# Expert loop of a pooled-attention and top-1 MoE kernel: another order of the four arms, an aligned loop head and a branch hint

## The chip, the cores and the metric

One core of one Trainium2 chip. The metric is device time in microseconds (us), the median of the timed runs. A profiled execution lies beside them, with a trace of each engine's instructions: PE (TensorE, the matrix engine), PEld (its weight loads, from the same sequencer), DVE (VectorE), ACT (ScalarE), POOL (GpSimd), SP (SyncE, here the issuer of most DMAs).

## The reference

Attention with keys and values averaged over groups of 8 positions, then a mixture of experts in which each token goes to its one best expert:

```python
k_p = k.reshape(B, H, Sp, pool, D).mean(axis=3)          # B, H, S, D = 8, 8, 576, 64; pool = 8
v_p = v.reshape(B, H, Sp, pool, D).mean(axis=3)
attn = softmax(scale * q @ k_p^T)
x = (attn @ v_p).transpose(0, 2, 1, 3).reshape(B * S, H * D)     # 4608 tokens of 512
expert_idx = argmax(x @ w_gate)                                   # 8 experts
for e in range(E):
    h = np.maximum(x_sorted[lo:hi] @ w1[e], 0.0)                  # 512 -> 1024
    y_sorted[lo:hi] = h @ w2[e]                                   # 1024 -> 512
return gate_w[:, None] * y_sorted[inv_perm]
```

(softmax and the sorting by expert are abridged.)

## The kernel before

The attention part, up to some 200 us, is written out in full; it scatters each token's row into a DRAM table `x_by_expert`, sorted by expert. The expert part works in blocks of up to 256 tokens of one expert. Its first block is computed in the straight code; all others run in a loop over `T` blocks, where `T` and a small table (`tabs`) come from the routing that was computed just before. Here the loop makes 21 passes.

Matmuls are done in float16 with values split into a high and a low part, three products for each float32 product. The weights of an expert, split likewise, lie in one of two slots: slot 0 (`w` in the trace) and slot 1 (`qt` for w1, `kv` for w2). Experts take the slots in turn. While the blocks of one expert are computed, the next one's weights are loaded into a staging buffer (by SP, `wwhole`) and split into the other slot (by ACT and DVE, `part` and `wsplit`, L116 and L118).

A block that holds at most 128 tokens does half the work. So there are four arms: slot 0 or 1, whole or half block. A table entry `code` picks one: 0 is slot 0 half, 1 is slot 0 whole, 2 is slot 1 half, 3 is slot 1 whole. Each arm is a call of `block(s, full, en)` and holds the code of PE, ACT and DVE for it; POOL and SP have no code in the arms. On PE an arm has the up part (`up`, lines L1005 to L1007: 96 matmuls of 256 columns, or 128 in a half block, into the PSUM tiles ps, pp and pq) and the down part (`finish`, L1082: 48 matmuls of 512 columns, or 24). Between them ACT makes the relu's high part (`relu_hi`, L1073) and DVE the low part (`relu_lo`, L1076). With them in each arm: DVE's copy of the next block's transposed tokens (`arrive`, L931), the split of the tokens of the block after it (`split_hi` and `split_lo`, L913 and L916), and ACT's scaled result (`take`, L1247), which POOL scatters to the output (`give`, L1252).

The order of the work within an arm is the order of the Python calls (the schedule is manual). The head of the loop body loads `code` and `en` into registers (L1221) and branches twice (L1309, in `either`). The loop is of the kind in which semaphores are never reset: waits compare with registers that count up. Its closing branch is L1314 in the trace, and each engine executes a prefetch hint for that branch (BRANCH_PREFETCH_HINT, shown under L1359) at the top of each pass.

Each engine has a sequencer that reads its instructions, executes branches, register operations and waits by itself, and hands the others to the engine. The trace has rows for both.

Of the kernel before, what the change touches and what calls it, by code (L numbers as in the profile page):

```python
# [15 lines left out]
ENG = mybir.EngineType  # L16
# [16 lines left out]
def kernel(  # L33
# [51 lines left out]
    def wwhole(e, stage):  # L85

        for src, dst in zip((w1d, w2d), WHOLE[stage]):
            src = src[e:e + 1] if isinstance(e, int) else src[ds(e, 1)]
            nc.sync.dma_start(dst, src.rearrange("e p c f -> p (e c) f"))
# [806 lines left out]
    def keep_ids(x=xg):  # L896
        pass_ids(gC, iC, x[:, :, ID + 1], x[:, :, ID].bitcast(I32))
        nc.gpsimd.tensor_tensor(x[:, :, ID].bitcast(I32), far.to_broadcast([128, 2]), zi.to_broadcast([128, 2]), op=OP.add)

    def move_ids():  # L900
        pass_ids(gA, iA, gC, iC)

    def take_ids():
        pass_ids(gB, iB, gA, iA)
# [13 lines left out]
    def split_x():  # L918
        split_hi()
        split_lo()  # L920
# [5 lines left out]
    def trans():  # L926
        nc.sync.dma_start(xTs.rearrange("p (c t) -> p c t", c=4 * DC), xh.rearrange("p j a t -> p (j a t)"),  # L927
                          transpose=True)

    def arrive():  # L930
        nc.vector.tensor_copy(xT.rearrange("p c (j t) -> p j c t", j=2),  # L931
                              xTs.rearrange("p (j c t) -> p j c t", j=2, c=2 * DC))
# [67 lines left out]
    def up(s, f, n):  # L1000
        dst = pH[f // 2][:, (f % 2) * BLK:(f % 2) * BLK + n]
        c = slice(f * 128, (f + 1) * 128)
        for d in range(DC):
            wh, wl = W1[s][0][:, d, c], W1[s][1][:, d, c]
            nc.tensor.matmul(dst, wh, xT[:, d, 0:n], start=(d == 0), stop=False)  # L1005
            nc.tensor.matmul(dst, wh, xT[:, DC + d, 0:n], start=False, stop=False)  # L1006
            nc.tensor.matmul(dst, wl, xT[:, d, 0:n], start=False, stop=(d == DC - 1))  # L1007
# [64 lines left out]
    def relu_hi(k, n=BLK):  # L1072
        nc.scalar.activation(pair(hT[0], k, n), ups_of(k, n), AF.Relu)  # L1073

    def relu_lo(k, n=BLK):
        V.scalar_tensor_tensor(pair(hT[1], k, n), ups_of(k, n), 0.0, pair(hT[0], k, n), op0=OP.max, op1=OP.subtract)  # L1076

    def finish(s, j, half):
        y = pY[j]
        for x, z in (((0, 0), (0, 1), (1, 0)), ((0, 0), (1, 0), (0, 1)))[half]:  # L1080
            for f in range(4 * half, 4 * half + 4):
                nc.tensor.matmul(y, hT[x][:, f, 128 * j:128 * j + 128], W2[s][z][:, f, :],  # L1082
                                 start=(half == x == z == f == 0), stop=(half == z == 1 and f == FC - 1))
# [6 lines left out]
    rest = [f for _, _, f in fillers]  # L1090
# [128 lines left out]
    def entry(kind, t, engines, lo, hi):  # L1219
        ap = tabs[kind:kind + 1, t:t + 1] if isinstance(t, int) else tabs[kind:kind + 1, ds(t, 1)]  # L1220
        return nc.values_load(ap, engines=engines, min_val=lo, max_val=hi)  # L1221

    def load_x(t, x=xg):
        row = entry(0, t, [ENG.SP], 0, E * SEG - 128)
        many = entry(4, t, [ENG.SP], 0, 3)

        def part(lo, n, dst):
            src = xs[ds(row + lo, n), :]
            st = nc.sync.dma_start(dst, src if n < BLK else src.rearrange("(j p) x -> p j x", p=128))
            if isinstance(t, int):  # L1230
                for e, o in padded:
                    if e > t + 1:
                        tc.declare_no_dep(st.ins, o.ins, reason="rows of later experts")

        with tc.If(many > 2) as cmp:
            part(0, BLK, x)
        with cmp.Else():
            part(0, 64, x[0:64, 0])
            with tc.If(many > 0):
                part(64, 64, x[64:128, 0])  # L1240
                with tc.If(many > 1):
                    part(128, 64, x[0:64, 1])
# [3 lines left out]
    def take(j):  # L1246
        nc.scalar.activation(ys[j], pY[j], AF.Copy, scale=gB[:, j:j + 1])  # L1247

    def give(j):
        nc.gpsimd.tensor_tensor(iG[:, 0:j + 1], iB[:, 0:j + 1], zi.to_broadcast([128, j + 1]), op=OP.add)  # L1250
        nc.gpsimd.tensor_tensor(spacer[:, 0:1], ys[j][0:1, 0:1], iG[0:1, j:j + 1].bitcast(F32), op=OP.add)  # L1251
        st = nc.gpsimd.indirect_dma_start(  # L1252
            out=out, out_offset=bass.IndirectOffsetOnAxis(ap=iG[:, j:j + 1], axis=0), in_=ys[j], in_offset=None,
            bounds_check=N - 1, oob_is_err=False)
        for o in given:
            tc.declare_no_dep(st.ins, o.ins, reason="rows of other tokens")
        given.append(st)
# [22 lines left out]
    T = nc.values_load(tab[0:1, 0:1], min_val=1, max_val=TMAX)  # L1280
# [4 lines left out]
    def part(s, en):  # L1285
        with tc.If(en > 0):
            for j in range(8):
                wsplit(1 - s, j, "hl", s)

    def block(s, full, en):  # L1290
        for h in range(2):
            n = BLK if full else 128
            for f in range(4 * h, 4 * h + 4):
                up(s, f, n)
            for k in (2 * h, 2 * h + 1):
                relu_hi(k, n)
                relu_lo(k, n)
        arrive()
        split_x()
        part(s, en)  # L1300
        if full:
            for half in range(2):
                finish(s, 1, half)
        take(1)
        for half in range(2):
            finish(s, 0, half)

    def either(c, f, g):
        with tc.If(c) as cmp:  # L1309
            f()  # L1310
        with cmp.Else():
            g()

    with tc.For_i(0, T, 1, iteration_sync="reg_based") as t:  # L1314
        code = entry(6, t, [ENG.PE, ENG.Activation, ENG.DVE], 0, 3)
        en = entry(2, t, [ENG.Activation, ENG.DVE], 0, 1)
        en3 = [entry(x, t, [ENG.SP], 0, E - 1) for x in (7, 3)]
        more = [entry(5, t + x, [ENG.SP], 0, 1) for x in (2, 3)]
        take_ids()
        move_ids()  # L1320
        keep_ids()
        nc.gpsimd.drain()
        either(code < 2,
               lambda: either(code > 0, lambda: block(0, True, en), lambda: block(0, False, en)),
               lambda: either(code > 2, lambda: block(1, True, en), lambda: block(1, False, en)))
        with tc.If(more[0] > 0):
            trans()
        with tc.If(more[1] > 0):
            load_x(t + 3)
        give(1)  # L1330
        for x in (0, 1):
            with tc.If(en3[x] > 0):
                wwhole(en3[x], 1 - x)
        take(0)
        give(0)
# [28 lines left out]
```

## Time and profile before

| | |
|---|---|
| timed runs, us | 617.01, 619.32, 626.0 (median 619.32) |
| profiled execution, us | 623.24 |
| its span, first to last instruction, us | 621.3 |
| PE busy | 573.8 us, 92% |
| DVE, ACT, POOL busy | 50%, 47%, 43% |
| loop, first to last matmul, us | 215.34 to 613.8 |
| mean granted clock of PE | 0.982 |

Busy time is the time in which an engine has an instruction in work; branches, waits and register operations don't count. Matmuls overlap in the pipeline: a row's duration is longer than the distance to the next one, and it is the distance from start to start that adds up. [...]

### The profile page before, as it was taken

The page shows a single profiled execution, that of the slowest core. Times are in us where ns is not written, and L with a number is a line of the kernel's source. Part 1 is how long each engine was busy: PE and PEld are TensorE (multiplying, and loading weights), DVE is VectorE, ACT ScalarE, POOL GpSimd, SP SyncE. Part 2 cuts the span into 40 slices and gives each one's busy share as a digit, 9 for nine tenths or more (in the row PEclk, how much of TensorE's full clock was granted, in tenths as well). Part 3 has the DMA queues.
Part 4 walks back from the last instruction along what each step waited for, and adds up shares of the span by engine and source line. Part 5 has one row for each costly group of instructions (what it writes and reads, how often), then busy time and mean ns, then how long its engine had stood idle before and what let it go on. Part 6 is the DMA issues. An engine that isn't in the chain of part 4 may idle for free. (4 is left out here: it accounts for less than half of the span.)

```text
span 621.3 us, 15783 instructions
## 1 busy us (share of the span) xinstructions
PE 573.8 (92%) x4721; PEld 420.5 (68%) x4722; DVE 313.1 (50%) x625; ACT 291.6 (47%) x648; POOL 269.9 (43%) x524
## 2 busy tenths in 40 slices
PE   6798889999887899998999999999999999999995
PEld 5787878888775366655667666767666666567663
DVE  6567888987965336224772772213722461222122
ACT  2487779899951135225652772223522441222122
POOL 5799398997986153211332332122311132111213
PEclk9699999999999799999999999999999989999999
DMA  8996698976397547954888579243332324321200
GB/s 233 309 307 206 220 294 290 294 242 218 120 310 208 140 106 211 399 132 92 266 250 269 168 249 338 72 106 80 77 89 51 87 55 106 89 51 53 68 17 31
DMA packets 96323, 107.15 MB, mean 172 GB/s; under 512 B 54430, under 2 KB 64670, under 8 KB 96288
## 3 DMA queue, kind: packets, MB, share of 16 engines
q1 hardware_dynamic: 89648, 85.72, 49.0%
q0 software_dynamic: 6640, 20.99, 9.2%
q8 instruction: 19, 0.31, 0.2%
q14 instruction: 16, 0.13, 0.1%
HBM read 72.99 MB, written 23.37 MB: 155 GB/s over the span
## 5 line engine op out<-in xcount | busy, mean ns | idle before, releaser
L1082 PEld LDWEIGHTS <-bd 128*128 128x128 f16 x936 | 91.6, 98 | 113.5 <-issue 7.9
L1251 POOL TENSOR_TENSOR spacer<-ql,iG 1x1 f32<-1x1 f32 x44 | 20.3, 462 | 206.1 <-ACT ql L1247 196.9
L1076 DVE SCALAR_TENSOR_TENSOR bd<-ps,bd 128x512 f16<-128x512 f32 (+1 forms) x44 | 27.5, 630 | 158.6 <-ACT bd L1073 154.8
L516 ACT ACTIVATE both<-ps,nmx 128x72 f32<-128x72 f32 x288 | 68.6, 327 | 12.8 <-DVE nmx L509 12.0
L1082 PE MATMUL po<-w,bd 128*128 128x512 f16 x264 | 58.9, 379 | 0.0
L1082 PE MATMUL po<-kv,bd 128*128 128x512 f16 x264 | 58.8, 379 | 0.0
L1073 ACT ACTIVATE bd<-ps 128x512 f16<-128x512 f32 (+1 forms) x44 | 24.0, 548 | 71.2 <-PE L1005 42.4
L1252 POOL DMA_INDIRECT out_dram<-ql,iG x44 | 46.2, 1049 | 21.4 <-issue 20.3
L1082 PE MATMUL pq<-w,bd 128*128 128x512 f16 x192 | 46.5, 394 | 4.4 <-issue 3.5
L1082 PE MATMUL pq<-kv,bd 128*128 128x512 f16 x216 | 48.1, 379 | 0.0
L499 PE MATMUL ps<-bd,qT 128*128 128x144 f32 x256 | 46.2, 305 | 1.6 <-DVE bd L785 0.9
L1005 PE MATMUL ps<-kv,qt 128*128 128x256 f16 (+1 forms) x176 | 45.6, 267 | 2.1 <-issue 2.1
L1007 PE MATMUL ps<-kv,qt 128*128 128x256 f16 (+1 forms) x176 | 45.7, 267 | 2.0 <-DVE qt L118 2.0
L1006 PE MATMUL ps<-kv,qt 128*128 128x256 f16 (+1 forms) x176 | 45.6, 267 | 0.0
L1007 PE MATMUL ps<-kv,w 128*128 128x256 f16 (+1 forms) x176 | 43.1, 258 | 1.9 <-DVE w L118 1.9
L1005 PE MATMUL ps<-kv,w 128*128 128x256 f16 (+1 forms) x176 | 43.1, 258 | 1.6 <-DVE kv L118 1.5
L1006 PE MATMUL ps<-kv,w 128*128 128x256 f16 (+1 forms) x176 | 43.1, 258 | 0.0
L1247 ACT ACTIVATE ql<-po,gB 128x512 f32<-128x512 f32 x22 | 15.0, 684 | 58.7 <-PE L1005 33.8
L709 POOL DMA_INDIRECT x_by_expert<-both,rpos x36 | 35.4, 985 | 14.7 <-issue 5.9
L1005 PEld LDWEIGHTS <-qt 128*128 128x128 f16 x352 | 34.7, 99 | 8.2 <-issue 2.6
L1007 PEld LDWEIGHTS <-qt 128*128 128x128 f16 x352 | 34.7, 99 | 7.3 <-issue 3.2
L1005 PEld LDWEIGHTS <-w 128*128 128x128 f16 x352 | 34.4, 98 | 6.3 <-ACT kv L116 2.0
(250 smaller groups left out, 1361.1 us busy)
## 6 DMA issues: line engine op xcount, KB each, us to landing
both<-in_moe_w_dram SPq DMA_DIRECT2D x6, 2048.0 KB, 11.6
st<-in_moe_w_dram SPq DMA_DIRECT2D x6, 2048.0 KB, 14.5
vb<-x_by_expert SPq DMA_DIRECT2D x16, 578.0 KB
st<-in_moe_w_dram SPq DMA_DIRECT2D x8, 1024.0 KB
kv<-in_k_dram SPq DMA_DIRECT2D x7, 1024.0 KB
kv<-in_v_dram SPq DMA_DIRECT2D x7, 1024.0 KB
qt<-in_q_dram SPq DMA_DIRECT2D x6, 1024.0 KB
qt<-in_q_dram SPq DMA_DIRECT2D x4, 512.0 KB
```

The costliest lines, as they stand in the source:

```text
L499: nc.tensor.matmul(ps[:, x * 2 * KP:(x + 1) * 2 * KP], t[:, h, :], BD[b % 3][:, :, h, :], start=True, stop=True)
L516: nc.scalar.activation(p[:, h * KP:(h + 1) * KP], ps[:, x * KP:(x + 1) * KP], AF.Exp, bias=nmx[:, x:x + 1], scale=-1.0)
L709: st = nc.gpsimd.indirect_dma_start(out=xs, out_offset=bass.IndirectOffsetOnAxis(ap=Z["pos"][:, u:u + 1], axis=0), in_=X[:, u, :], in_offs ...
L1005: nc.tensor.matmul(dst, wh, xT[:, d, 0:n], start=(d == 0), stop=False)
L1006: nc.tensor.matmul(dst, wh, xT[:, DC + d, 0:n], start=False, stop=False)
L1007: nc.tensor.matmul(dst, wl, xT[:, d, 0:n], start=False, stop=(d == DC - 1))
L1073: nc.scalar.activation(pair(hT[0], k, n), ups_of(k, n), AF.Relu)
L1076: V.scalar_tensor_tensor(pair(hT[1], k, n), ups_of(k, n), 0.0, pair(hT[0], k, n), op0=OP.max, op1=OP.subtract)
L1082: nc.tensor.matmul(y, hT[x][:, f, 128 * j:128 * j + 128], W2[s][z][:, f, :], start=(half == x == z == f == 0), stop=(half == z == 1 and f ...
L1247: nc.scalar.activation(ys[j], pY[j], AF.Copy, scale=gB[:, j:j + 1])
L1251: nc.gpsimd.tensor_tensor(spacer[:, 0:1], ys[j][0:1, 0:1], iG[0:1, j:j + 1].bitcast(F32), op=OP.add)
L1252: st = nc.gpsimd.indirect_dma_start(out=out, out_offset=bass.IndirectOffsetOnAxis(ap=iG[:, j:j + 1], axis=0), in_=ys[j], in_offset=None, b ...
```

## The change

The choice among the four arms is made in another order: first whether `code` is 1 (whole block of slot 0), and only otherwise among the other three. In the code the three other arms come first (slot 0 half, slot 1 half, slot 1 whole), and the whole-block arm of slot 0 comes last, directly in front of the loop's end. The branch that leads to it gets the label "rest". At the head of the body PE executes a hint for that branch, whose value is computed from the pass number: `(t + 63) // 64` is 0 in the first pass ("likely taken") and 1 in all later ones ("likely not taken"). And the first instruction of the loop body on PE is placed at the start of a block of instruction fetch. What the arms compute, and the order within an arm, stay as they are. The order of the arms changes for PE, ACT and DVE; the hint and the alignment are for PE alone.

```diff
-    def either(c, f, g):
-        with tc.If(c) as cmp:
+    def either(c, f, g, label=None):
+        with tc.If(c, label=label) as cmp:
             f()
         with cmp.Else():
             g()
 
-    with tc.For_i(0, T, 1, iteration_sync="reg_based") as t:
+    with tc.For_i(0, T, 1, iteration_sync="reg_based", head_align_engines=[ENG.PE]) as t:
+        tc.mark_branch_hint_location("rest", hint=(t + 63) // 64, engines=[ENG.PE])
         code = entry(6, t, [ENG.PE, ENG.Activation, ENG.DVE], 0, 3)
...
-        either(code < 2,
-               lambda: either(code > 0, lambda: block(0, True, en), lambda: block(0, False, en)),
-               lambda: either(code > 2, lambda: block(1, True, en), lambda: block(1, False, en)))
+        either(code != 1,
+               lambda: either(code < 1, lambda: block(0, False, en),
+                              lambda: either(code < 3, lambda: block(1, False, en), lambda: block(1, True, en))),
+               lambda: block(0, True, en), "rest")
```

## Rows read from the trace of the kernel before

**Rows 1.** The page: busy us of each engine (share of the span), instructions.

```profile
PE 573.8 (92%) x4721; PEld 420.5 (68%) x4722; DVE 313.1 (50%) x625; ACT 291.6 (47%) x648; POOL 269.9 (43%) x524
```

**Rows 2.** Stages of the loop: length, busy us (instructions), PE clock, DMA share, GB/s.

```profile
215.34:236.20 20.86, 20.86 (x144) 13.97 (x144) 8.79 (x10) 9.68 (x13) 8.48 (x18) 1.00 0.54 116
...
237.88:258.71 20.83, 20.83 (x144) 14.08 (x145) 7.89 (x9) 5.57 (x9) 7.98 (x16) 1.00 0.91 329
...
281.85:293.39 11.54, 11.51 (x120) 7.90 (x121) 4.78 (x8) 5.36 (x9) 1.99 (x9) 1.00 0.22 63
293.39:316.38 22.99, 21.36 (x145) 13.88 (x144) 19.06 (x20) 17.44 (x22) 6.32 (x14) 1.00 0.89 259
316.38:326.90 10.52, 10.52 (x121) 7.69 (x120) 5.81 (x9) 3.97 (x7) 5.56 (x12) 1.00 0.80 258
```

**Rows 3.** Waits of PE, 209 to 300 us, then 300 to 621 us: total, times, longest.

```profile
PE ps L1005 <- issue: 2.1, 1, 2.1
PE ps L1007 <- DVE w L118: 1.6, 3, 0.6
PE ps L1005 <- DVE kv L118: 1.5, 1, 1.5
...
PE ps L1007 <- DVE qt L118: 2.0, 4, 0.5
```

**Rows 4.** PE's branches, windows 232:233 and 277.7:278: ns min/median/max, first and last start.

```profile
L1309 PEldq COMPARE_BRANCH  x1: 3549/3549/3549, 232.3 to 232.3; - x1
...
L1309 PEldq COMPARE_BRANCH  x2: 366/2012/3659, 277.4 to 277.8; - x2
```

**Rows 5.** The same view: 283:611 (both lines), 254:255 and 491:493.

```profile
L1309 PEldq COMPARE_BRANCH  x50: 71/186/228, 291.3 to 601.6; - x50
...
L1314 PEldq COMPARE_BRANCH  x17: 231/231/245, 290.0 to 599.9; - x17
...
L1309 PEldq COMPARE_BRANCH  x1: 202/202/202, 254.8 to 254.8; - x1
...
L1309 PEldq COMPARE_BRANCH  x1: 186/186/186, 491.9 to 491.9; - x1
```

**Rows 6.** DMA queues 212:232, 232:237, 277:283.5 (packets, MB, share), first of 283.5:621.

```profile
q8 instruction: 2, 0.03, 0.7%
...
q8 instruction: 1, 0.02, 1.6%
...
q8 instruction: 2, 0.03, 1.9%
...
q1 hardware_dynamic: 43296, 33.16, 35.9%
```

**Rows 7.** PE's sequencer at loop entry, and its hints in all passes.

```profile
L1314 PEldq COMPARE_BRANCH  x1: 376/376/376, 212.5 to 212.5; - x1
...
L1309 PEldq COMPARE_BRANCH  x2: 71/87/103, 214.3 to 214.4; - x2
...
L1359 PEldq BRANCH_PREFETCH_HINT  x21: 31/36/52, 212.9 to 600.2; - x21
```

**Rows 8.** PE in time, fourth pass: start us, us, what [idle before].

```profile
281.85 0.22 PE L1005 MATMUL ps<-kv,qt 128*128 128x128 f16 x1 [2.14 <-issue]
...
283.52 0.22 PE L1005 MATMUL ps<-kv,qt 128*128 128x128 f16 x1
...
284.19 0.22 PE L1005 MATMUL ps<-kv,qt 128*128 128x128 f16 x1
```

**Rows 9.** PE in time, loop entry, and the end of a half block of slot 0.

```profile
213.77 1.46 PE L1082 MATMUL po<-w,bd 128*128 128x512 f16 x6
215.34 0.28 PE L1005 MATMUL ps<-kv,w 128*128 128x256 f16 x1
...
494.61 0.27 PE L1005 MATMUL ps<-kv,qt 128*128 128x256 f16 x1
```

**Rows 10.** ACT in time, the first relu of the loop.

```profile
218.34 0.60 ACT L1073 ACTIVATE bd<-ps 128x512 f16<-128x512 f32 x1 [2.39 <-PE L1005]
```

## Prediction

> **What bounds the kernel now.** I read the page first: PE is busy 92% of a 621.3 us span, every other engine 50% or less [rows 1]. So time is worth looking for only where PE stands still, and the change touches nothing before the loop, so only in the loop. The stage table comes next [rows 2]. A whole block (144 matmuls) takes 20.83 us, a half block (120, of which 96 are half as wide) 10.5 us, PE busy from edge to edge. The 21 passes sum up with few exceptions: a hole of 1.7 us after the first pass (236.20 to 237.88 us), one of 2.14 us after the third [rows 8], a fourth pass (half block) of 11.54 us instead of 10.52 us, and waits for split weights, in the pass from 293.39 us and once more later [rows 3].
>
> What ends the two holes? The waits of PE name "issue" for the 2.1 us one and DVE's split of the next expert's weights for the 1.5 us one [rows 3]. The second name is wrong: the pass from 237.88 us reads slot 0 (w), while DVE is splitting into slot 1. The sequencer's branches tell more. PE's sequencer runs ahead of the array; it takes the branch at the end of the first pass's arm at 232.3 us, while the array works on until 236.2 us, and that branch lasts 3549 ns. In the fourth pass the branch at 277.8 us, into the half-block arm of slot 1, lasts 3659 ns [rows 4]. The 50 later branches of these lines last 71 to 228 ns, the 17 later back edges 231 to 245 ns [rows 5]. The DMA view says what the two long ones are: in their stretches the instruction queue q8 moves one and two pieces of 16 KB, and from 283.5 us to the end it moves none: that stretch's list begins with q1 and has data queues alone [rows 6]. So code is fetched once; each first far jump into a part of the loop that is not there yet stops the sequencer for some 3.6 us, and after the fourth pass everything is there.
>
> The durations also give the order of the code now. In the first pass both choosing branches are short (71 and 103 ns [rows 7]), so they fall through: the whole-block arm of slot 0 follows the head. Its end jumps over the three other arms. The taken ones last 186 to 230 ns.
>
> **The change, part by part.** All terms are differences of PE's time in the profiled execution (623.24 us with 621.3 us of span).
>
> *Arm of slot 0 moved to the loop's end.* The first three passes run it. Its end now runs on into the loop's end, as code in sequence, which the trace shows arriving without a stop (in the first pass q8 brings two pieces before 232 us, and no hole appears). The miss at 232.3 us goes. Worth: first pass to second 237.88 - 215.34 = 22.54 us, against 20.83 us for the second: -1.71 us.
>
> *Half-block arms first.* The arm that the fourth pass enters now begins some 260 instructions behind the head (the half-block arm of slot 0, 120 weight loads and 120 matmuls, lies between, and its waits), so in the piece behind the head's, and is fetched in sequence when the head is first entered, as the piece behind the head is now. (A piece holds some 230 instructions or more: the loop took five, and its four arms have 2 x 288 + 2 x 240 loads and matmuls, besides waits and branches [rows 2, 6].) Then the miss at 277.8 us goes as well: 281.85 - 258.71 = 23.14 us against 20.83 us, -2.31 us. The fourth pass is slow for the same reason: with the sequencer's lead used up, its first twelve products take 1.67 us (281.85 to 283.52), the next twelve 0.67 us [rows 8]. With the lead kept it should take 10.52 us, not 11.54 us: -1.02 us. Sum of the three: -5.04 us. Does this reach the end? The next waits, at 293 us, are for weights whose split follows the fourth pass's relus on ACT and DVE, so they move along with PE; no wait of PE in the loop names a DMA [rows 3]. I count all of it.
>
> *The price: the first pass must now jump to the far end.* The arm lies behind three others, and the miss comes at 214.3 us instead. Its excess is 3549 - 202 = 3.35 us or 3659 - 228 = 3.43 us [rows 4, 5]; take 3.4 us. There is no cover: the first matmul of the loop starts at 215.34 us, 0.27 us after the array could have taken it [rows 9], so the sequencer is already last. What it gets back is the added hint. No row shows what a hint saves; the bounds are nothing (3.4 us stay) and all of it (0). I take the time between: the hint stands behind the first instruction of the body (212.9 us), the branch it speaks of at 214.3 us [rows 7], a lead of 1.4 us, 0.2 us of it gone for the arithmetic in front of the hint. So 3.4 - 1.2 = 2.2 us. The arithmetic, two register instructions and a hint at about 0.1 us each from start to start, adds 0.3 us; one branch fewer on the way (71 ns and its gap) takes off 0.15 us. Entry: +2.35 us.
>
> *Aligned head.* The padding in front is jumped over once. At the entry there is a branch of 376 ns already [rows 7]. Between nothing and one more miss of 3.4 us, if the piece with the moved head has not come yet; nearest is the row just named, which is no miss, so 0.
>
> *Each later pass.* The hint's 0.3 us lies in the sequencer's lead. From the end of the 3549 ns branch (235.9 us) to the next matmul (237.88 us) the head takes 2.0 us. After a whole block the arm's end comes at 254.85 us, plus 0.2 and 2.0 gives 257.05 us, and the array needs its next work at 258.71 us: 1.66 us spare. After the half block of slot 0 it is 491.9 + 0.19 + 2.0 = 494.1 us against 494.61 us [rows 5, 9]: 0.5 us spare. That is the tight place, and it always leads to the whole-block arm of slot 1, which now stands behind three branches instead of two (two of them taken, as the second tests code < 1 and the third code < 3): +0.3 us. With the hint 0.6 us, so 0.1 us short, three times. If the lead is wholly lost there, the first products go as in rows 8, about 1 us each: between 0 and +3 us. I take +0.2 us, since one of the three, that from 494.61 us, waits for weights anyway.
>
> *ACT and DVE* take the new order without hints. Should their sequencers miss 3.4 us in the first pass as PE's does, ACT's first relu (218.34 us, after 2.39 us of waiting for PE [rows 10]) is 1 us late at most against PE, whose first product is late as well, and relus have a third of the pass to catch up: 0.
>
> Sum: -5.04 + 2.35 + 0.2 = -2.5 us, 623.24 to 620.7 us. The profiled execution lies 3.9 us above the median of the timed runs, 619.32 us (617.01 to 626.0); on the median the forecast is **616.8 us**.
>
> **The rivals.**
> *The hint does its work fully* (the far arm arrives in time): entry +0.15 us, sum -4.7 us, 614.6 us. For it: nothing measured. Against it: 1.2 us of lead against a fetch of 3.5 us.
>
> *The misses stay.* The hint does nothing, or the request for the far arm takes the place of the piece behind the head, so that the fourth pass still misses: -1.71 + 3.4 + 0.15 + 0.2 + 0 to 1 = +2.0 to +3.0 us, 622 us; with the first alone, -1.3 us, 618 us. For it: two pieces would be wanted at once at the loop's head, and both misses now occur at first jumps out of sequence.
>
> *Slower: the back edge loses its hint.* Each pass begins with a hint for the loop's closing branch (21 of them [rows 7]); the new one follows at once, and from the second pass on it says "not taken". If a sequencer holds a single hint and the head's piece isn't kept, the back edge misses in each of 20 turns. After the 16 whole blocks the price is 3.4 - 1.66 = 1.7 us, after four half blocks 3.4 - 0.5 = 2.9 us: 27.2 + 11.6 = 39 us, 656 us, +6%. It decides as soon as the loop's pieces don't all stay. Against it stand the rows without fetches: with two slots and both kinds of arm used in turn from 293 to 603 us, q8 moved nothing [rows 6], so the pieces stay without any hint, and the new order makes the loop no longer. [...]
>
> **How the numbers follow.** Forecast 55%, misses stay 25%, hint complete 15%, back edge lost 5%. A measurement of this kernel tells about 2% (12.4 us) from no change; the first three cases lie within 5 us and so within it. Faster by over 2% is left to the scatter of the runs (3%); slower by over 2% is the last rival and a little scatter (6%); within 2%: 91%. The range takes in the cases from 614.6 to 622 us and some of the spread of the runs, which reached 2.3 us below and 6.7 us above their median: 612 to 624 us.
>
> **What would show it.** PE's branch rows: the miss at the first pass's arm end and the one into the fourth pass's arm gone; one of some 2.4 us at about 214.5 us; the first matmul of the loop near 217.7 us, later passes 20.83 us apart, the first half block 10.5 us. q8 moves nothing after the fourth pass. The prediction is wrong if branches of over 1 us recur in later passes, if the fourth pass still begins with a hole, or if a slower clock after the entry's hole lengthens the first pass; after the 2.14 us hole now, the clock stayed 1.00 [rows 2].

## The result, and the profile after

The changed kernel takes 625.21 us (median of 22 runs, 619.34 to 975.9) against 619.67 us for the kernel before on the same chip (22 runs, 616.53 to 626.0). The ratio is 1.0055, 95% interval 1.003 to 1.008: slower by some 3.4 us, where 2.5 us of gain were forecast. Executions more than 1.5% above the fastest of their kernel, 975.9 us among them, are left out of the ratios but not of the medians, so the two need not agree. The profiled execution of the changed kernel took 633.56 us and is one of its longest; it is read here for where time goes, and a second one (span 621.4 us) follows with the experiments.

The page: PE's busy time grew from 573.8 to 580.0 us with the same number of matmuls [rows 1], so some of them ran slower.

```profile
PE 580.0 (92%) x4721; PEld 425.1 (67%) x4722; DVE 312.8 (50%) x625; ACT 292.1 (46%) x648; POOL 269.7 (43%) x524
```

The stage table, for the first, second, fourth, fifth, sixth, seventh and eighth pass (length, busy of PE, PEld, DVE, ACT, POOL, PE clock, DMA share, GB/s), answers to [rows 2]; the two lines behind "..." are the half-clock stretch at the start of the first pass, and of the fifth.

```profile
219.27:241.77 22.50, 22.50 (x144) 14.89 (x145) 11.37 (x13) 11.60 (x14) 7.70 (x19) 0.92 0.39 88
241.77:262.60 20.83, 20.83 (x145) 14.07 (x144) 6.89 (x9) 4.83 (x7) 7.68 (x16) 1.00 0.97 352
283.46:294.36 10.90, 10.90 (x121) 7.68 (x119) 3.85 (x7) 5.12 (x9) 2.54 (x10) 1.00 0.20 59
297.03:319.50 22.47, 22.47 (x144) 14.74 (x145) 17.34 (x19) 15.82 (x20) 6.60 (x13) 0.92 0.85 253
319.50:330.10 10.60, 10.60 (x121) 7.61 (x119) 5.86 (x9) 3.28 (x6) 5.89 (x12) 1.00 0.90 287
336.38:360.00 23.62, 23.62 (x144) 15.52 (x145) 11.34 (x13) 11.60 (x14) 0.93 (x6) 0.88 0.36 84
360.00:380.90 20.90, 20.90 (x146) 14.10 (x145) 13.73 (x16) 12.29 (x15) 6.11 (x14) 1.00 0.82 270
...
219.32:222.73 3.41, 3.41 (x17) 2.35 (x18) 0.00 (x0) 0.00 (x0) 2.31 (x3) 0.50 0.62 179
...
297.83:301.20 3.37, 3.37 (x19) 2.17 (x17) 3.37 (x4) 3.37 (x5) 0.38 (x1) 0.50 0.30 52
```

Three holes stand out, ahead of 219.27, 297.03 and 336.38 us. The pass behind each is longer than 20.83 us: at its start, or 0.8 us behind it in the fifth pass, the granted clock is 0.50 of full speed for 3.4 us; at the seventh it is 0.50 for 6.8 us, the first 1.0 us of them still in the hole. PE in time shows the holes in brackets, and what the profile names as their releaser [rows 8, 9]:

```profile
219.27 0.36 PE L1005 MATMUL ps<-kv,w 128*128 128x256 f16 x1 [3.32 <-issue]
...
297.03 0.27 PE L1005 MATMUL ps<-kv,w 128*128 128x256 f16 x1 [2.51 <-ACT w L116]
...
336.38 0.37 PE L1005 MATMUL ps<-kv,qt 128*128 128x256 f16 x1 [6.14 <-issue]
```

The releaser of the second, ACT's split, is again not the cause. PE's sequencer has a long choosing branch ahead of each of the three, and nowhere else; the end of the first pass's arm, 3549 ns before [rows 4], is now an ordinary back edge of 235 ns. The views are the loop's lines in windows at 215, 293, 329, 361 to 625 and 238 us, then the hints (42, two in each pass), and all back edges, that of the first pass included [rows 5, 7]:

```profile
L1309 PEldq COMPARE_BRANCH  x1: 4042/4042/4042, 215.1 to 215.1; - x1
...
L1309 PEldq COMPARE_BRANCH  x1: 3208/3208/3208, 293.7 to 293.7; - x1
...
L1309 PEldq COMPARE_BRANCH  x3: 88/366/6187, 329.2 to 329.7; - x3
...
L1309 PEldq COMPARE_BRANCH  x44: 70/169/236, 378.6 to 621.7; - x44
...
L1361 PEldq BRANCH_PREFETCH_HINT  x42: 38/43/55, 213.6 to 611.0; - x42
...
L1314 PEldq COMPARE_BRANCH  x20: 213/219/240, 238.0 to 610.4; - x20
```

The instruction queue of the DMA view [rows 6], in windows 214:225, 225:283, 283:284, 294:300, 330:345 and 345:358 (packets of 16 KB, MB, share). From 358 to 600 us it moves nothing; the view of that stretch has only data queues, of which the first is the last line here:

```profile
q8 instruction: 3, 0.05, 2.0%
...
q8 instruction: 1, 0.02, 0.1%
...
q8 instruction: 1, 0.02, 8.4%
...
q8 instruction: 1, 0.02, 1.0%
...
q8 instruction: 2, 0.03, 0.9%
...
q8 instruction: 2, 0.03, 1.2%
...
q1 hardware_dynamic: 30864, 20.60, 32.3%
```

Ten pieces, where the loop before took five up to the fourth pass and none later. One starts in each of the three long branches, 0.97, 1.02 and 3.73 us after the branch begins. By the places of the arms (an estimate, below), the whole arm of slot 0 was fetched at the entry and its first piece again at 294.7 us.

The account from pass to pass, start to start of the first matmuls, after less before: hole at the entry +3.2 us (3.48 against 0.28), first pass +1.65, hole behind it -1.69, hole behind the third pass -2.3, fourth pass -0.64, hole ahead of the fifth +2.67, fifth pass -0.48, hole ahead of the seventh +6.3, seventh pass +2.67, all the rest -1.66 (most of it a later wait for weights that shrinks as PE comes later). Sum +9.7 us; the loop, from the end of the straight code's block to the end of the last pass, takes 408.7 us against 398.9. "Loop time" means this stretch from here on: the straight block ahead of it varies between executions of one and the same code (27.9 to 39.6 us over all profiles), which single spans mix in.

### The profile page after: what moved, and what is told of

Same layout as the page of the kernel before. It is cut to its first block, busy times and chain, and to the rows that moved or that the text cites. A ratio compares the mean times of both kernels' runs of the same rounds, so it can differ in the third digit from the quotient of the medians.

```text
span 631.8 us, 15812 instructions
## 1 busy us (share of the span) xinstructions
PE 580.0 (92%) x4721; PEld 425.1 (67%) x4722; DVE 312.8 (50%) x625; ACT 292.1 (46%) x648; POOL 269.7 (43%) x524
## 4 chain that ended last, share of the span: by engine, by line
PE 68%; ACT 11%; DVE 8%; issue 4%; DMA 3%; POOL 3%; another core or an unknown queue 1%; ACTq 1%; SPq 1%; POOLq 0%; DVEq 0%; PEld 0%; PEldq 0%
PE po L1082 15%; PE pq L1082 14%; PE ps L1005 6%; PE ps L1007 5%; PE ps L1006 5%; ACT both L516 3%; PE pp L1005 3%; PE pp L1007 3%; PE pp L1006 3%; PE pq L1005 3%; PE pq L1007 2%; PE pq L1006 2%; PE po L560 2%; ACT ph L528 2%; PE pp L523 2%
## 5 line engine op out<-in xcount | busy, mean ns | idle before, releaser
L1251 POOL TENSOR_TENSOR spacer<-ql,iG 1x1 f32<-1x1 f32 x44 | 23.5, 535 | 218.3 <-ACT ql L1247 210.1
L1252 POOL DMA_INDIRECT out_dram<-ql,iG x44 | 43.7, 994 | 21.6 <-issue 20.5
L1005 PE MATMUL ps<-kv,qt 128*128 128x256 f16 (+1 forms) x176 | 46.1, 270 | 6.1 <-issue 6.1
L1005 PE MATMUL ps<-kv,w 128*128 128x256 f16 (+1 forms) x176 | 45.2, 270 | 5.8 <-issue 3.3
L1007 PE MATMUL ps<-kv,qt 128*128 128x256 f16 (+1 forms) x176 | 46.1, 270 | 1.9 <-DVE qt L118 1.9
L1006 PE MATMUL ps<-kv,qt 128*128 128x256 f16 (+1 forms) x176 | 46.1, 270 | 0.0
L1006 PE MATMUL ps<-kv,w 128*128 128x256 f16 (+1 forms) x176 | 45.3, 270 | 0.0
L1007 PE MATMUL ps<-kv,w 128*128 128x256 f16 (+1 forms) x176 | 45.2, 270 | 0.0
```

Source lines behind the costliest of these rows:

```text
L1252: st = nc.gpsimd.indirect_dma_start(out=out, out_offset=bass.IndirectOffsetOnAxis(ap=iG[:, j:j + 1], axis=0), in_=ys[j], in_offset=None, b ...
```

## The experiments

The loop's code on PE is about 1160 instructions by a count of its rows in the trace. An estimate from the pieces that came (four at the entry of chain, below, beside the head's own) puts it at five pieces of 16 KB. The arms of ACT and DVE were moved as well, but in before and after none of their branches in the loop lasts over 0.15 us (at most 146 ns on DVE and 119 ns on ACT, in after); only PE's long branches come with holes. By the same estimate, in the order of the change the third arm lies in the third and fourth piece, and the whole arm of slot 0 fills the rest of the fourth and reaches into the fifth. Passes run slot 0 whole three times, then slot 1 half, slot 0 whole, slot 0 half, and in the seventh slot 1 whole.

**Parts of the change alone.** All four on one chip (before: 620.05 us, 18 runs).

no_hint leaves out the hint and its label:

```diff
-        tc.mark_branch_hint_location("rest", hint=(t + 63) // 64, engines=[ENG.PE])
```

> The changed kernel without the added hint (new order of the arms and aligned head stay). Theory A (the order alone does it: jumps to far pieces of code bring them out of sequence, and pieces that are needed again are dropped): a branch of about 3.5 us at the loop's entry, and again branches of over 3 us in the fifth and seventh pass, with instruction fetches on q8 after the fourth pass; time as the changed kernel, ratio to before 1.003 to 1.008. Theory B (the added hint does it: it displaces the hint for the back edge, an unneeded piece behind the loop is fetched at the loop's end, and that pushes needed ones out): entry branch about 3.5 us, then no branch above 0.4 us and no fetch on q8 after the fourth pass; 3.4 us paid at the entry and 5.0 us saved, ratio 0.995 to 0.999.

no_align leaves out `head_align_engines=[ENG.PE]`, and keeps the hint.

> The changed kernel without the aligned head (new order and hint stay). Theories A and B: as the changed kernel, ratio 1.003 to 1.008, since the first fetch after the entry follows the loop's first instruction by 1.36 us in both profiles, so the head was at a fetch boundary before already. Theory C (the alignment does it): no misses after the fourth pass, ratio 0.996 to 1.000.

after_again and before_again are the two kernels once more.

> The changed kernel once more, for a second profile. If the later misses follow from the order of fetches alone (A or B), they stand in the same passes, five and seven; if they depend on chance in what is dropped, in others or not at all. Ratio 1.003 to 1.008.

> The kernel before once more, for a second profile. All theories: ratio 1.000, misses of some 3.6 us at the end of the first pass's arm and at the entry of the fourth pass's arm, and no fetch on q8 afterwards. If what is dropped is chance: misses in other passes too.

order_only, on another chip (before: 617.25 us, 29 runs), leaves out both.

> The new order of the arms alone, without hint and without aligned head. Theory A (the order does it): an entry branch of some 4 us, one or two more branches of 3 to 7 us in the passes four to seven with fetches on q8, ratio to before 1.005 to 1.013 like the two kernels that lack one part each. If hint and alignment were needed together for the loss: 0.995 to 1.000.

| | median us (n) | ratio, 95% | long PE branches in the profile, ns | loop us |
|---|---|---|---|---|
| no_hint | 624.42 (7) | 1.0069 [1.0040, 1.0097] | entry 4176, fifth pass 3239, seventh 6556 | 406.8 |
| no_align | 628.43 (6) | 1.0131 [1.0098, 1.0163] | entry 4022, end of fourth pass's arm 4897 | 402.8 |
| after_again | 625.65 (6) | 1.0069 [1.0045, 1.0093] | entry 4022, end of fourth pass's arm 4867 | 402.8 |
| before_again | 623.39 (12) | 0.9991 [0.9957, 1.0025] | end of first pass's arm 3479, into fourth pass's arm 4287 | 399.6 |
| order_only | 622.56 (12) | 1.0067 [1.0024, 1.0109] | entry 3956, fifth pass 3739, seventh 5602 | 405.7 |

The order alone makes the late branches, and in order_only a loss of the same size; its second run (order_again, below) has the branches too, but its ratio of 1.0021 [0.9978, 1.0064] doesn't tell a loss from none. How far medians wander is seen in before_again, the same code as before: 3.3 us above it by the median, 0.9991 by the ratio. The entry's branch lasts 4.0 to 4.2 us with the hint (4042, 4022 and 4022 ns) and without (4176 and 3956 ns): the hint saves nothing there. And the new order has two later patterns: either the fifth and the seventh pass miss, or only the end of the fourth pass's arm does. after and after_again are one kernel and show one each, so which comes is not set by the code alone. (The expectation for after_again, if the order of fetches alone decided, was the same passes.) The first pattern was traced mostly in long executions (after 633.56 us, no_hint 633.09, order_again 621.3, each the longest or second longest of its kernel), but order_only's, 623.34 us, lies near its median. The second pattern in after_again, DMA queue q8 in windows 210:225, 276:281 and 286.5:293.5; then the branch at 286.7 us; then PE in time:

```profile
q8 instruction: 4, 0.07, 1.9%
...
q8 instruction: 1, 0.02, 1.4%
...
q8 instruction: 3, 0.05, 4.4%
...
L1309 PEldq COMPARE_BRANCH  x1: 4867/4867/4867, 286.7 to 286.7; - x1
...
293.65 0.27 PE L1005 MATMUL ps<-kv,w 128*128 128x256 f16 x1 [4.05 <-DVE w L118]
```

Its account against before: entry +3.2, first pass +1.65, the two old holes -4.0, fourth pass -1.0, hole at its end +4.2, rest -0.2: +3.9 us of loop time, which is the size of the measured ratio. The releaser that PE in time names, DVE's split, is wrong a third time: the branch ends at 291.6 us.

What the hint costs shows in small holes after half blocks of slot 0: 0.12 to 0.17 us, two or three times each in after, after_again and no_align, against 0 to 0.04 us in no_hint and order_only. In far_hint, below, q8 moves three pieces from 220 to 240 us, in before two (at 228.76 and 233.24 us). For no_align nothing in the trace explains a ratio above that of after_again.

**Hints at other places.** far_hint is the kernel before with a hint (always taken) at the start of slot 0's whole arm, for the branch into the arm that the fourth pass enters:

```diff
+            if s == 0:
+                tc.mark_branch_hint_location("h1", engines=[ENG.PE])
...
-               lambda: either(code > 2, lambda: block(1, True, en), lambda: block(1, False, en)))
+               lambda: either(code > 2, lambda: block(1, True, en), lambda: block(1, False, en)), "h1")
```

> The kernel before (its order, no alignment) with one hint more on PE: at the start of the whole-block arm of slot 0, for the branch that enters the half-block arm of slot 1, fixed at taken. So this hint is executed some 60 us before the fourth pass's miss, and in the two passes between. If a hint has the target fetched as soon as it is executed: one more fetch on q8 early in the first pass, the branch into the fourth pass's arm at most 0.4 us, no hole there, ratio 0.992 to 0.997. If a hint has no effect so far ahead, or none at all: the miss of 3.6 us stays, ratio 0.998 to 1.002.

Ratio 1.0010 [0.9965, 1.0055]; both misses stay (3421 and 3323 ns), though the hint ran in all three passes ahead of the second, the one that it speaks of.

skip_hint puts a hint into the same piece of code as its branch. skip_nohint is the control. `last` holds the last 24 matmuls of the arm, which the call of `block` with False leaves out.

```diff
+        with tc.If(code == 1):
+            block(0, True, en, False)
+        with tc.If(code == 1):
+            tc.mark_branch_hint_location("skip", engines=[ENG.PE])
+            last(0)
+        with tc.If(code != 1, label="skip"):
+            either(code < 1, lambda: block(0, False, en),
+                   lambda: either(code < 3, lambda: block(1, False, en), lambda: block(1, True, en)))
```

> Order of before with the whole arm of slot 0 first, its last 24 matmuls under a branch of their own, then a branch that jumps past the other three arms; a hint (likely taken) for that branch stands at the start of the last part, in the same 16 KB of code as the branch, some 5 us ahead of it. Theory (a piece of code comes when the piece before it has been at work for about a us, or on demand; this hint brings nothing): the branch at the end of the first pass's arm still lasts 3.2 to 4.3 us, as in before, and the time is that of skip_nohint within 1 us. Rival (a hint brings the target's code, but only when the sequencer already works in the piece of the branch): a fetch on q8 within 2 us of the hint, the branch under 0.4 us, and 1.7 us of PE's waiting less than in skip_nohint.

> As skip_hint, without the hint: the control. Both theories: the branch at the end of the first pass's arm lasts 3.2 to 4.3 us; in the fourth pass, the first that leaves the arm of slot 0, one more branch of that length, either at its start or at the end of its arm. Time within 4 us of before.

In skip_hint the hint runs at 224.0 us and the branch comes at 228.7 us. Its hint, the branch, then q8 in 223:226 and 229:231:

```profile
L1368 PEldq BRANCH_PREFETCH_HINT  x1: 41/41/41, 224.0 to 224.0; - x1
...
L1332 PEldq COMPARE_BRANCH  x1: 3349/3349/3349, 228.7 to 228.7; - x1
...
q8 instruction: 1, 0.02, 1.8%
...
q8 instruction: 1, 0.02, 3.5%
```

One piece comes near the hint, but it isn't the branch's target: skip_nohint fetches a piece at the same point of the pass (13.2 us after the pass's first matmul, here 13.1), and its branch lasts 3620 ns. The target is fetched only after the branch has begun, at 229.5 us. So the theory held for the hint. Three expectations did not hold. The second long branch, in the fourth pass, came in neither kernel. The times lie 1.9 us apart, not within 1 us, with the hint on the slower side. And they lie far from before: the two take 691.01 and 689.12 us, ratios 1.112 and 1.111. Here three branches stand in a row instead of a choice of one, and the profile puts most of PE's waits at the passes' starts to the sequencers of DVE and ACT at these lines. PE's waits in skip_nohint:

```profile
PE ps L1005 <- DVEq L1327: 15.8, 3, 8.7
PE ps L1005 <- issue: 14.6, 5, 4.9
PE ps L1005 <- ACTq L1327: 13.6, 5, 3.6
PE ps L1005 <- DVEq L1331: 7.1, 2, 4.8
```

**Other orders.** near_order is the kernel before with slot 1's half arm placed second (slot 0 whole, slot 1 half, slot 0 half, slot 1 whole); near_again is its second run. swap_half is the changed kernel with the two half arms exchanged, so that the fourth pass's arm follows the head; swap_again its second run.

> The kernel before with another order of the arms and nothing else: slot 0 whole directly behind the head (as before), then slot 1 half, slot 0 half, slot 1 whole, which is the order in which the passes first come to them (passes 1, 4, 6, 7). Theory D (a miss comes from a first jump to a piece that was not the next in sequence, and pieces brought in sequence stay): only the miss at the end of the first pass's arm is left (about 3.5 us, a hole of 1.7 us); the branch into the fourth pass's arm takes at most 0.4 us, the fourth pass 10.5 us; 2.3 + 1.0 us less than before, ratio 0.992 to 0.997. Theory E (pieces are lost by chance, whatever the order): a branch of over 3 us in some pass after the first, ratio 0.997 to 1.004.

> The same kernel as near_order once more, to see what its typical run holds. Theory (piece after piece): two long branches of 3.2 to 4.9 us, at the end of the first and of the fourth pass's arm, none later, loop time 397 to 402 us, as in before; then its time against before is within 1%. Rival (this order costs something that is not code): loop time over 402 us with the same two branches.

> The changed kernel with its two half-block arms exchanged: slot 1 half directly behind the head, then slot 0 half, slot 1 whole, slot 0 whole last; hint and alignment as in the change. The fourth pass's arm then ends within the second piece of the loop and does not run into the third, as it does in the change. Theory D: the entry's miss of 4 us stays, with slower clock behind it; no branch over 1 us in the passes four and five, at most one at the sixth pass's arm, which is now the first to run into the third piece; 2 to 5 us less than the changed kernel, ratio to before 0.997 to 1.003. Theory E or any cause in the far jump of the first pass alone: misses in passes four and five as in the change, ratio 1.005 to 1.010.

> The same kernel as swap_half once more. Theory: one long branch alone, of about 4 us, at the loop's entry, four pieces of code fetched later without a wait, loop time 399 to 402 us; the time would lie 0 to 4 us above before. Rival (the fourth pass's order leaves a second miss in some executions, or the loop waits longer for weights): a second branch over 3 us, or a wait for the split weights of over 2 us in the fifth pass, loop time over 403 us.

| | median us (n) | ratio, 95% | long PE branches in the profile, ns | loop us |
|---|---|---|---|---|
| near_order | 622.22 (12) | 1.0086 [1.0046, 1.0127] | end of first pass's arm 3209, of fourth's 3589 | 399.4 |
| near_again | 623.80 (10) | 1.0035 [1.0002, 1.0069] | the same two, 3925 and 3671 | 400.1 |
| swap_half | 627.01 (6) | 1.0182 [1.0129, 1.0236] | entry 4030 | 400.9 |
| swap_again | 625.99 (4) | 1.0120 [1.0045, 1.0195] | entry 3997 | 399.9 |

In near_order the miss into the fourth pass's arm goes, as placing it behind the head should do, and one at that arm's end comes in its place (3589 ns), at the jump to the loop's end, which had been long at the first pass's end too (3209 ns). In swap_half nothing is missed after the entry: four pieces come later (q8 at 316.3, 331.0, 340.3 and 346.5 us), and no branch of the choice lasts over 361 ns. So near_order's expectation of one miss failed, and its time did too; the other three have the branches that were expected of them. The times of the swap kernels don't follow from the branches: loop time at most 2 us above before's 398.9 and 399.6, but 7 and 11 us by the ratio (for near_order and near_again at most 1.2 us, and 2 and 5 us). Both swap profiles are the shortest of their runs, so what lengthens the other executions is in no trace here.

**Is it the jump over code, or the amount of code?** Fetch times alone leave open whether pieces came again because of the amount of code, or because the entry jumped over those between. chain and chain_swap keep order_only's arms and change the choice: each arm's test stands at its head and jumps to the next head, so the way to the last arm leads through the pieces between. (chain_swap has slot 1's half arm first.)

```diff
-        either(code != 1,
-               lambda: either(code < 1, lambda: block(0, False, en),
-                              lambda: either(code < 3, lambda: block(1, False, en), lambda: block(1, True, en))),
-               lambda: block(0, True, en))
+        either(code < 1, lambda: block(0, False, en),
+               lambda: either(code == 2, lambda: block(1, False, en),
+                              lambda: either(code > 2, lambda: block(1, True, en), lambda: block(0, True, en))))
```

> The order of the arms after the change (half slot 0, half slot 1, whole slot 1, whole slot 0), without hint and alignment; but the choice is a chain: each arm's test stands at its head and jumps to the next arm's head, so the way to the last arm leads through the code pieces between. Theory (a piece is fetched behind the one at work; a jump over pieces puts the far one where they belong): one to three long branches at the loop's entry, 4 to 11 us of PE's waiting together instead of 3.5, and no branch over 1 us in any later pass; loop time 393 to 402 us, against 405.7 in order_only. Rival (the memory doesn't hold all five pieces): the entry as said, and branches over 3 us in the fifth and seventh pass as before, loop time 405 to 413 us.

> As chain, with the half arm of slot 1 first and that of slot 0 second (the fourth pass then runs the arm that lies nearest to the head). Theory: as chain, no long branch after the entry, loop time within 2 us of chain. Rival (the memory doesn't hold all pieces): a branch over 3 us in a pass from the fifth on.

> The same kernel as order_only once more, on the chip of the two chains: the control with the jump. Both theories: a long branch of about 4 us at the entry, and then either two (fifth pass, 3.2 to 3.8 us; seventh, 5.6 to 6.6 us) or one at the end of the fourth pass's arm (4.9 us); loop time 402 to 407 us.

All three on one chip (before: 614.78 us, 19 runs). chain has three long branches at the entry and none over 0.3 us in the 20 later passes. Its choosing branches at the entry (window 206:211, which takes in the one from 203.1 us) and from 214 us on, and its back edges; PE's waits, 205 to 621 us; q8 in 200:211 and 211:218; and from 218 to 606 us the DMA view's data and other queues, in which q8 has no line:

```profile
L1309 PEldq COMPARE_BRANCH  x3: 2994/3472/3649, 203.1 to 210.3; - x3
...
L1309 PEldq COMPARE_BRANCH  x66: 74/210/247, 233.5 to 603.8; - x66
...
L1314 PEldq COMPARE_BRANCH  x21: 86/232/241, 232.1 to 604.2; - x21
...
PE ps L1005 <- issue: 9.5, 1, 9.5
...
q8 instruction: 3, 0.05, 1.7%
...
q8 instruction: 1, 0.02, 0.9%
...
q1 hardware_dynamic: 53025, 43.86, 39.9%
q0 software_dynamic: 3211, 8.71, 5.9%
q14 instruction: 1, 0.01, 0.0%
```

chain_swap is alike (2604, 4034 and 2930 ns at the entry, nothing later). The loops take 403.4 and 403.5 us, 1.4 us above the top of what was expected, since the entry's hole (9.65 us) came out near its bound and the first pass ran its start at half clock (+1.45 us). The control with the jump misses in the fifth and seventh pass again, as expected; its entry branch is longer than the 4 us expected, and its loop 0.3 us above the range. Its branches up to 330 us, and PE's waits:

```profile
L1309 PEldq COMPARE_BRANCH  x14: 73/208/7179, 203.5 to 319.4; - x14
...
PE ps L1005 <- issue: 11.3, 2, 6.5
PE ps L1005 <- ACT w L116: 1.8, 1, 1.8
```

(entry 7179, fifth pass 3459, seventh 5676 ns; loop 407.3 us). So in chain no piece came for 388 us, with the same arms in the same order and 20 passes through them, and the later misses go with the jump. In time chain is no gain: 617.44 us (10), ratio 1.0074 [1.0035, 1.0113], which fits its 403.4 us of loop; chain_swap 618.75 us (4), 1.0106 [1.0021, 1.0191]; order_again 615.79 us (10), 1.0021 [0.9978, 1.0064]. The profiled execution of order_again, at 621.3 us, is the longest of its ten, so its typical execution loses less than the one traced.

## Why the prediction was wrong

*What bounds the kernel* was read rightly: only holes of PE in the loop moved, and long branches of its sequencer made them.

*The gains.* First pass's arm end: -1.71 us forecast, -1.69 measured. The miss into the fourth pass's arm: -2.31, and -2.30 measured. The fourth pass with its lead kept: -1.02, and -0.64 measured in after, -1.0 in after_again, no_hint and order_only (10.54 us).

*The entry* was mis-sized: +2.35 us forecast, +4.85 measured. The 1.2 us that the hint was to give back are nothing in every run with and without it, and the first pass began at half clock (+1.65 us), which the prediction had named as a way to be wrong and counted at 0 because the clock had stayed 1.00 after a hole of 2.14 us [rows 2, 8]. This hole was 3.3 us. With this term alone the sum would be -5.04 + 4.85 + 0.2, nothing gained and nothing lost. The rest is the next step.

*The step that failed* is "So code is fetched once; each first far jump ... stops the sequencer for some 3.6 us, and after the fourth pass everything is there", and with it, under the rival of the back edge, "so the pieces stay". Rows 6 showed this for the order before. In the new order pieces come again, ten in after against five in before, and more branches are long: +4.2 us at the end of the fourth pass's arm (after_again, no_align), or +2.67 and +6.3 us ahead of the fifth and seventh pass and more half clock (after, no_hint, order_only, order_again). With the +4.2 us of after_again the sum comes to some +4.2 us, and its loop was traced 3.9 us longer. The kernel before already held the sign, and the prediction passed over it: by the estimated places of the arms, the loop's fifth piece, fetched for the jump at 232.3 us, came again at 282.3 us, which [rows 6] counted as one of two pieces in 277:283.5 without asking which.

The q8 times show when pieces came. In after they start at 214.98 us (1.36 us after the loop's first instruction), 216.04 (in the entry's branch), 219.83, 228.78, 283.41, 294.67 (in the fifth pass's branch, from 293.65), 333.47 (in the seventh's, from 329.74), 338.61, 349.98 and 357.12 us. Which piece each one is can only be estimated, from the places of the arms and the arm that PE was in: 216.04 and 219.83 us the fourth and fifth, for the far arm of slot 0; 283.41 us the third, at the half arm of slot 1; 294.67 us the fourth again; 333.47, 338.61 and 349.98 us the third, fourth and fifth again, for the whole arm of slot 1 and what lies behind it; 228.78 and 357.12 us none that an arm needs. No run shows by what rule a piece that had come was fetched again. That it goes with the way in, and not with the amount of code, is shown by chain (no branch over 247 ns after the entry) against order_again (3459 and 5676 ns). Nor does a run show why one kernel has two patterns.

*The tight place* after half blocks of slot 0: +0.2 us forecast; the small holes of 0.12 to 0.17 us and a following pass longer by 0.2 us, twice outside a wait for weights, make some +0.8 us in after_again. *The aligned head* at 0: agreed as to the entry, where the first fetch follows the head's first instruction by 1.4 us in both kernels; no_align's time is not explained.

*The rivals.* "The hint does its work fully" falls. "The back edge loses its hint" falls as well: 20 back edges of 213 to 240 ns. "The misses stay" was nearest, with the hint doing nothing as it said, but its sum of 622 us left out the clock and every miss behind the fourth pass's start, and the miss into the fourth pass's arm that it allowed for did not occur. No hint fetched a target ahead of its branch: the piece came 0.97 us after the branch began in after, and 0.8 us after in skip_hint; far_hint's branch still lasted 3323 ns.

*Open:* why no_align, swap_half and swap_again, and less so near_order, take longer than their profiles say, and how often each pattern comes in executions without a trace. swap_half, with no late branch after the entry, has the highest ratio of all orders with nested choices, so the times of whole executions don't by themselves show that the later misses make the loss of 3.4 us; the traced loops show the misses and what each cost.

## What to carry to other kernels

When arms of a loop are reordered, don't count only which first jumps go: follow the order in which the passes enter the pieces of code, since here the jump over pieces cost its own miss at once (4042 ns in after) and two more later (3208 and 6187 ns), where chain, which leads through the pieces, has three at its entry and none after it. Before "it is fetched once" is relied on, look at which piece each fetch brings, above all for one that came twice. The miss at the loop's entry had no lead to hide in (4042 ns, a hole of 3.32 us in after), and a clock of 0.50 for 3.4 us followed the hole; the miss at the end of a long arm hid half of itself (3549 ns, a hole of 1.7 us in before).

## What the runs showed of the hardware

- A missed branch lasted 2.6 to 4.9 us, and five lasted 5.6 to 7.2 us, all where the DMA share is 1.01 or more: in after, from 329.7 to 333.4 us, it is 1.03 at 405 GB/s, and the instruction queue's piece starts only at 333.5 us. The other four, in no_hint, order_only and order_again, stand in stretches of 1.01 to 1.04. A full share alone doesn't make them: in chain it is 1.11 from 203.06 to 204.0 us, and the piece for the branch of 3472 ns starts there 0.9 us after the branch.
- Behind the entry's hole of 3.5 to 4.0 us the granted clock of PE was 0.50 for 3.4 us in after, after_again, no_hint, order_only and swap_half (first pass +1.66 us), but not in no_align, behind 3.46 us, nor in swap_again, behind 3.38 us, whose first passes took 20.84 us. It fell behind shorter holes too: 2.5 us in after (fifth pass) and, in before, at 499.45 us behind four waits of 0.4 to 0.5 us, where it had stayed 1.00 behind 2.14 us.
- A hint for a branch saved nothing at leads of 1.2 us (4042 ns with it, 4176 without), 4.7 us (3349 and 3620) and, in far_hint, from some 21 to 63 us ahead (3323 ns, against 3659 and 4287 in the two profiles of before).
- Three branches in sequence that PE, ACT and DVE execute cost some 68 us here (skip_nohint against before on the same chip); the profile puts 36.5 us of PE's waits to the sequencers of DVE and ACT at them, and names none of these in before.
